# Weight preparation gets an order behind the operand splits on VectorE (attention and two MLPs, Trainium2)

## Chip, cores and metric

The kernel runs on one core of a Trainium2 chip. The metric is the device time of one execution in microseconds (us).

## What is computed

Attention over pooled keys and values, then two MLPs. The weights arrive as float64, whose bits the kernel decodes to float32; the rest is float32:

```python
k_p = k.reshape(B, H, Sp, 8, D).mean(axis=3)          # v_p alike; B = H = 8, S = 576, D = 64
attn = softmax(q @ k_p^T / sqrt(D))
x  = (attn @ v_p) -> [4608, 512]
x  = leaky_relu(x @ w_in1, 0.01) @ w_out1             # 512 -> 2048 -> 512
out = relu(x @ w_in2)**2 @ w_out2                     # 512 -> 2048 -> 512
```

## The kernel before

A float32 product is made from three matmuls of rounded operands: each operand is split into a high part (a cast on ScalarE, ACT) and a low part (operand minus high part, on VectorE, DVE), and `three()` (L302 to L304) multiplies high by high, high by low and low by high. So every operand of TensorE (PE) costs one ACT and one DVE instruction ahead of it: `split_weights` (L229, L230), `first` (`gh` L826, `gl` L827) and `split_into` (`oh`, `xh` L886; `ol`, `xl` L887).

Work runs in two stages.

**Stage 1: 80 units** (t, f). The first MLP is done plainly for the first 2304 tokens: five tiles t (four of 512 tokens, the last of 256) by 16 blocks f of hidden columns. Unit (t, f) traces `first` for the following unit, the weight splits, and `second`. Attention is interleaved (`advance`, three or five of its steps per unit) and is traced to its end in unit (3, 5). Two side jobs ride along:

- `prepare_sums` (`sums1`): 16 sets of sums of the first MLP's weights, two steps each (32 steps; L250 to L254), needed in stage 2. One step is traced in every odd unit from tile 1 on.
- `prepare_products` (`prep`): the second MLP's weights, 16 products (8 `in`, 8 `out`). A product has these steps: fetch; decode (ACT L192, then DVE L194 and L197, then L201, then L211, which is two half-size instructions in two steps for `out`); sums (four DVE instructions L250 to L254); high and low parts (ACT L291, DVE L292). That is 7 steps for `in`, 8 for `out`, 120 in all. Once attention has been traced, each unit takes three steps from `sums1`, and when that is exhausted from `prep` (one step per unit in tile 4, f < 6).

**Stage 2: nine passes** of 768 tokens with a seven-product (Strassen-like) scheme; passes 0 to 2 still belong to the first MLP, 3 to 8 are the second. A pass has two halves, `first2` and `second2`, of 28 **hooks** each. A hook is one product of one block: 12 matmuls in a half of passes 0 to 2. In a hook, `next_block` splits weight sums for blocks up to two hooks ahead (L940 ACT, L941 DVE); `second2` splits, after the matmuls of product k, block a, the operand that product k+1, block a needs four hooks later (`split_g`: L886, L887, for products 6 and 4 with a `minus` L890 ahead of them), and once per product a step of `products_x` for the next pass (`xl` L887, `xs` L890). `first2` calls `split_g` once in seven hooks. After each hook of number not divisible by 3 a step of `prep` is traced; the second MLP's first weight block may not be fetched before `prep` is exhausted.

The order on each engine is made ahead of time by a planner: of the instructions that its clock sees as ready it takes the one traced earliest. An instruction traced late therefore runs early wherever an engine is otherwise free. `add_manual_dep` with `NoSync` adds an edge to this plan, so that one instruction stands behind another on the same engine; it puts no semaphore wait into the program.

Of the kernel before, what the change touches and what calls it, by code (L numbers as in the profile page):

```python
# [20 lines left out]
TT = 512  # L21
# [6 lines left out]
def raw(ap):  # L28

    return ap.bitcast(F32)  # L30
# [3 lines left out]
def attention_two_mlps(  # L34
# [11 lines left out]
    nc = tc.nc  # L46
# [20 lines left out]
    WIDE = [min(TT, PLAIN - at) for at in range(0, PLAIN, TT)]  # L67
    NTILE = len(WIDE)
    NQ = NF // 2
# [37 lines left out]
    def behind(mark, n):  # L107

        traced, (end, last) = nc.cur_bb.bb.instructions, mark
        for ins in traced[end:end + n]:  # L110
            if ins.engine in last:
                tc.add_manual_dep(
                    ins, last[ins.engine].name,
                    mybir.DependencyInfo(mybir.DependencyClass.NoSync, mybir.DependencyReason.DATA),
                    reason="behind",
                )

    def temp(name, dt=F32):
        return tpool.tile([P, TT], dt, tag="t", name=name)

    def work(name, n=TT, early=False):
        if early:
            return ps_a.tile([P, n], F32, tag="acc", name=name)
        return ps_w.tile([P, n], F32, tag="w", name=name)
# [35 lines left out]
    def tick(n=1):  # L160

        for one in LATE:
            one[0] -= n
        while LATE and LATE[0][0] <= 0:
            nc.sync.dma_start(**LATE.pop(0)[1])
# [90 lines left out]
    def prepare_sums():  # L256

        for p in range(NQ):
            for kind in ("in", "out"):
                b = [[W[kind, p + i * NQ][:, j * HD:(j + 1) * HD] for j in range(2)] for i in range(2)]  # L260
                if kind == "out":
                    b = [[b[j][i] for j in range(2)] for i in range(2)]
                s = spool.tile([P, 4, HD], F32, tag="stage", name=f"s1_{kind}{p}")
                yield from sum_steps(s, *b[0], *b[1])
                later(2, out=WS[1, kind, p // 2][:, :, p % 2].rearrange("o p x -> p o x"), in_=s)
                yield
# [32 lines left out]
    def three(outp, a, b, first, last, **kw):  # L299

        (ah, al), (bh, bl) = a, b
        nc.tensor.matmul(outp, ah, bh, start=first, stop=False, **kw)  # L302
        nc.tensor.matmul(outp, ah, bl, start=False, stop=False, **kw)  # L303
        nc.tensor.matmul(outp, al, bh, start=False, stop=last, **kw)  # L304
# [478 lines left out]
    def put_stores(until):  # L783

        while STORES and STORES[0][0] <= until:
            nc.sync.dma_start(**STORES.pop(0)[1])
# [10 lines left out]
    def load_x(t):  # L797
        XS[t] = []
        for c in range(NK):
            st = temp(f"xs1_{t}_{c}")[:, :WIDE[t]]  # L800
            nc.sync.dma_start(out=st, in_=x0[t][c * P:(c + 1) * P, :])
            XS[t].append(st)

    def split_x(t):
        new_x(t)
        for (hi, lo), st in zip(X[1, t], XS.pop(t)):
            nc.scalar.copy(hi, st)
            nc.vector.tensor_tensor(out=lo, in0=st, in1=raw(hi), op=ALU.subtract)
# [4 lines left out]
    def first(t, f):  # L813

        x = X[1, t]
        wh, wl = HL.pop(("in", t, f))
        n = WIDE[t]
        h = work(f"h1_{t}_{f}")[:, :n]
        for c in range(NK):
            cs = slice(c * P, (c + 1) * P)  # L820
            three(h, (wh[:, cs], wl[:, cs]), x[c], c == 0, c == NK - 1)
        g = temp(f"g1_{t}_{f}")[:, :n]
        nc.scalar.activation(g, h, AF.Prelu, alpha=0.01)
        gh = gpool.tile([P, TT], F32R, tag="gh", name=f"gh1_{t}_{f}")[:, :n]
        gl = gpool.tile([P, TT], F32R, tag="gl", name=f"gl1_{t}_{f}")[:, :n]
        nc.scalar.copy(gh, g)  # L826
        nc.vector.tensor_tensor(out=gl, in0=g, in1=raw(gh), op=ALU.subtract)  # L827
        G[t, f] = (gh, gl)

    A = {}  # L830
# [11 lines left out]
    def second(t, f):  # L842
        gh, gl = G.pop((t, f))
        wh, wl = HL.pop(("out", t, f))
        if f == 0:
            A[t] = [ps_a.tile([P, TT], F32, tag="acc", name=f"acc1_{t}_{j}")[:, :WIDE[t]] for j in range(4)]
        acc = A[t]
        for j in range(4):
            js = slice(j * P, (j + 1) * P)
            three(acc[j], (wh[:, js], wl[:, js]), (gh, gl), f == 0, f == NF - 1)  # L850
        if f == NF - 1:
            for j in range(4):
                o = temp(f"o1_{t}_{j}")[:, :WIDE[t]]
                if j % 2 == 0:
                    nc.scalar.copy(o, acc[j])
                else:
                    nc.vector.tensor_copy(o, acc[j])
                store_x1(t, j, o)
# [26 lines left out]
    def split_into(hi, lo, src):  # L885
        nc.scalar.copy(hi, src)  # L886
        nc.vector.tensor_tensor(out=lo, in0=src, in1=raw(hi), op=ALU.subtract)  # L887

    def minus(out_, a, b):
        nc.vector.tensor_tensor(out=out_, in0=a, in1=b, op=ALU.subtract)  # L890
# [56 lines left out]
    def split_g(t, a, prod):  # L947

        g11, g12, g21, g22 = GF[t, a]
        src = {1: g11, 2: g21, 3: g22, 4: g11, 5: g11, 6: g11, 7: g12}[prod]  # L950
        if prod == 6:
            minus(g11, g22, g11)
        elif prod == 4:
            minus(g11, g21, g11)
        hi, lo = (gopool.tile([P, 2, HT], F32R, tag=g, name=f"{g}2_{t}_{a}_{prod}") for g in ("oh", "ol"))
        split_into(hi, lo, src)
        GO[t, a, prod] = (hi, lo)

    def square(g):
# [133 lines left out]
    prep, preparing, hooks = None, True, 0  # L1093
    sums1 = prepare_sums()

    def advance():
        nonlocal at_work, made
        made += 1
        if next(att, 1):
            at_work = False  # L1100
        put_stores(made - 2 if at_work else made)

    x2pool, xg = None, iter(())
    for i, (t, f) in enumerate(units):
        if f == NF - 3 and t + 1 < NTILE:
            while ready[0] * S < min((t + 2) * TT, PLAIN):
                advance()
            put_stores(made)
            load_x(t + 1)
        if f == NF - 1 and t + 1 < NTILE:  # L1110
            split_x(t + 1)

        rate = RATES[min(t, 1)]
        if i + 1 < len(units):
            first(*units[i + 1])
        tick()
        if i + 2 < len(units):
            split_weights("in", *units[i + 2])
        if i + 1 < len(units):
            split_weights("out", *units[i + 1])  # L1120
        while at_work and made < due + rate // 2:
            advance()
        second(t, f)
        tick()
        due += rate
        while at_work and made < due:
            advance()
        if w1 < NF:
            prepare_weights(w1)
            w1 += 1  # L1130
        elif t > 0 and f % 2:
            next(sums1, None)
        if not at_work:
            if prep is None:
                ppool = ctx.enter_context(tc.tile_pool(name="prep", bufs=1, side="right", reuse_waits="tile"))
                prep = prepare_products()
            for _ in range(3 if WIDE[t] == TT else 1 if f < NQ - 2 else 0):
                if preparing and next(sums1, 1) and next(prep, 1):
                    preparing = False
        if i == NF:  # L1140
            behind(marks[0], 3000)
        if t == NTILE - 1 and f >= NQ - 2:
            if x2pool is None:
                assert not at_work and next(sums1, 1)
                w_early_stack.close()
                x2pool = ctx.enter_context(tc.tile_pool(name="x2", bufs=1, side="right", reuse_waits="tile"))
                ring = ctx.enter_context(tc.tile_pool(name="ring", bufs=RING, side="right", reuse_waits="tile"))
                load_x2(0)
                tick(9)
                blocks.insert(0, next_block())  # L1150
            else:
                if not XO:
                    xg = products_x(0)
                next(xg, None)
# [7 lines left out]
    for t in range(LEAD + NPASS):  # L1162
        lead[0] = t < LEAD
        for half in (first2, second2):
            if half is second2 and t + 1 < LEAD + NPASS:
                load_x2(t + 1)
            for _ in half(t):
                tick()
                hooks += 1
                if hooks % 3 and preparing and next(prep, 1):  # L1170
                    preparing = False
                    tick(9)


# [27 lines left out]
```

## Time and profile before

| | us |
|---|---|
| median of 3 runs | 1655.0 (1651.8 to 1656.2) |
| the profiled execution | 1653.7 |
| its span, first to last instruction | 1652.0 |
| busy PE | 1612.2 (98%) |
| busy DVE | 1365.2 (83%) |
| busy ACT | 992.2 (60%) |
| busy POOL | 117.3 (7%) |

The shares are means over stages. A busy PE is one with a matmul under way; since records of matmuls overlap, the pace is read from their count in a window. Idle PE is where a term of the end time can be looked for.

### The profile page before, as it was taken

What the parts mean: (1) busy time and instruction counts of PE and PEld (TensorE: products, weight loads), DVE (VectorE), ACT (ScalarE), POOL (GpSimd) and SP (SyncE); (2) the same over time, 40 slices, a digit from 0 to 9 for tenths busy, and PEclk for the clock granted to TensorE, in tenths of its full rate; (3) what the DMA queues carried; (4) which work ended last, traced back from release to release, by engine and by line L of the source; (5) the groups of instructions that cost most, each with busy time, mean ns of one, the idle gap of its engine ahead of it and who ended that gap; (6) DMA issues with size and microseconds to landing.
All of it is one profiled execution on the core that took longest, in us unless ns stands there. A gap on an engine that the chain in (4) does not pass through costs nothing.

```text
span 1652.0 us, 27801 instructions
## 1 busy us (share of the span) xinstructions
PE 1612.2 (98%) x10040; PEld 1523.0 (92%) x10040; DVE 1365.2 (83%) x2057; ACT 992.2 (60%) x1779; POOL 117.3 (7%) x149
## 2 busy tenths in 40 slices
PE   5999999999999999999999999999999999999998
PEld 5777788888888999999999999999999999999998
DVE  5899899878689999978759589689689599698695
ACT  5778655655667868667556546456456455465454
POOL 3121232123210000000000000000000000000000
PEclk8999999999999999999999999999999999999999
DMA  7766556766347778886666755765766657556554
GB/s 180 200 191 183 170 168 189 232 193 200 120 143 268 273 251 286 280 297 214 226 194 204 236 184 168 261 195 176 245 188 205 225 175 240 197 176 212 188 187 140
DMA packets 223722, 341.07 MB, mean 206 GB/s; under 512 B 56160, under 2 KB 138080, under 8 KB 223584
## 3 DMA queue, kind: packets, MB, share of 16 engines
q1 hardware_dynamic: 223264, 338.76, 64.4%
q8 instruction: 80, 1.31, 0.3%
q10 hardware_dynamic: 320, 0.52, 0.1%
q14 instruction: 58, 0.48, 0.1%
HBM read 268.44 MB, written 69.21 MB: 204 GB/s over the span
## 4 chain that ended last, share of the span: by engine, by line
PE 82%; DVE 10%; DMA 3%; ACT 3%; issue 2%; SPq 1%; DVEq 0%; ACTq 0%
PE acc L302 13%; PE h L302 13%; PE acc L303 13%; PE acc L304 13%; PE h L304 13%; PE h L303 13%; PE s L532 1%; DVE gl L827 1%; DVE hl_in L230 1%; DMA xs<-x 1%; ACT x L549 1%; DVE hl_out L230 1%; DMA st_in_out<-in_moe_w_out_dram 1%; PE trq L511 1%; PE pt L582 1%
## 5 line engine op out<-in xcount | busy, mean ns | idle before, releaser
L302 PE MATMUL h<-xh,wb_in 128*128 128x384 f32 x1008 | 337.1, 334 | 0.9 <-DVE g L999 0.9
L303 PE MATMUL h<-xl,wb_in 128*128 128x384 f32 x1008 | 336.7, 334 | 0.0
L304 PE MATMUL h<-xh,wb_in 128*128 128x384 f32 x1008 | 336.7, 334 | 0.0
L886 ACT CAST oh<-g 128x768 fp32r<-128x768 f32 x252 | 210.5, 835 | 152.1 <-PE acc L303 89.6
L302 PE MATMUL acc<-wb_out,oh 128*128 128x256 f32 x1008 | 282.1, 280 | 0.0
L304 PE MATMUL acc<-wb_out,ol 128*128 128x256 f32 x1008 | 281.4, 279 | 0.0
L303 PE MATMUL acc<-wb_out,oh 128*128 128x256 f32 x1008 | 281.2, 279 | 0.0
L887 DVE TENSOR_TENSOR ol<-g,oh 128x768 fp32r<-128x768 f32 x252 | 239.3, 951 | 32.3 <-ACT oh L886 32.0
L302 PEld LDWEIGHTS h<-xh,wb_in 128*128 128x128 f32 x1008 | 189.2, 188 | 1.6 <-DVE g L999 1.4
L304 PEld LDWEIGHTS acc<-wb_out,ol 128*128 128x128 f32 x1008 | 189.4, 188 | 0.0
L303 PEld LDWEIGHTS h<-xl,wb_in 128*128 128x128 f32 x1008 | 189.2, 188 | 0.0
L304 PEld LDWEIGHTS h<-xh,wb_in 128*128 128x128 f32 x1008 | 189.2, 188 | 0.0
L302 PEld LDWEIGHTS acc<-wb_out,oh 128*128 128x128 f32 x1008 | 189.1, 188 | 0.0
L303 PEld LDWEIGHTS acc<-wb_out,oh 128*128 128x128 f32 x1008 | 188.7, 187 | 0.0
L941 DVE TENSOR_TENSOR wb_in<-wb_in 128x512 fp32r<-128x512 f32 x144 | 98.7, 687 | 91.4 <-ACT wb_in L940 87.0
L940 ACT CAST wb_in<-wb_in 128x512 fp32r<-128x512 f32 x144 | 89.2, 622 | 139.9 <-DMA wb_in<-ws_in 139.4
L890 DVE TENSOR_TENSOR g<-g,g 128x768 f32<-128x768 f32 x144 | 136.4, 950 | 1.8 <-ACT g L961 1.3
L302 PE MATMUL h<-xh,hl_in 128*128 128x512 f32 (+1 forms) x320 | 123.2, 385 | 7.1 <-ACT hl_in L229 5.6
L302 PE MATMUL acc<-gh,hl_out 128*128 128x512 f32 (+1 forms) x320 | 121.3, 386 | 2.8 <-ACT gh L826 2.8
L304 PE MATMUL h<-xh,hl_in 128*128 128x512 f32 (+1 forms) x320 | 119.8, 374 | 0.8 <-DVE hl_in L230 0.7
L303 PE MATMUL acc<-gl,hl_out 128*128 128x512 f32 (+1 forms) x320 | 118.8, 374 | 0.7 <-DVE gl L827 0.7
L303 PE MATMUL h<-xl,hl_in 128*128 128x512 f32 (+1 forms) x320 | 119.4, 373 | 0.0
(156 smaller groups left out, 3289.7 us busy)
## 6 DMA issues: line engine op xcount, KB each, us to landing
wb_in<-wd_in SPq DMA_DIRECT2D x108, 512.0 KB, 4.0
wb_out<-wd_out SPq DMA_DIRECT2D x108, 512.0 KB, 4.2
wb_in<-ws_in SPq DMA_DIRECT2D x144, 256.0 KB, 2.7
wb_out<-ws_out SPq DMA_DIRECT2D x144, 256.0 KB, 2.7
xs<-x SPq DMA_DIRECT2D x18, 768.0 KB, 4.7
out_dram<-o SPq DMA_DIRECT2D x24, 384.0 KB, 3.3
q<-in_q_dram SPq DMA_DIRECT2D x32, 256.0 KB, 4.2
v<-in_v_dram SPq DMA_DIRECT2D x64, 128.0 KB, 3.7
```

The source lines that it names most:

```text
L230: nc.vector.tensor_tensor(out=lo, in0=w, in1=raw(hi), op=ALU.subtract)
L302: nc.tensor.matmul(outp, ah, bh, start=first, stop=False, **kw)
L303: nc.tensor.matmul(outp, ah, bl, start=False, stop=False, **kw)
L304: nc.tensor.matmul(outp, al, bh, start=False, stop=last, **kw)
L511: nc.tensor.transpose(tr[:, m, :n], t[:n, 2 * m:2 * m + 2].rearrange("p a d -> p (a d)"), ident[:n, :n])
L532: nc.tensor.matmul(sc[:n, 2 * m:2 * m + 2].rearrange("p a x -> p (a x)"), qT[:, 2 * e + m, :n], kT[b % 2][:, 2 * e + m].rearrange("p a x - ...
L549: nc.scalar.activation(x[:n, 4 * e + h], sc[:n, h], AF.Exp, bias=mx[:n, h], accum_out=sm[:n, 4 * e + h],)
L886: nc.scalar.copy(hi, src)
L887: nc.vector.tensor_tensor(out=lo, in0=src, in1=raw(hi), op=ALU.subtract)
L890: nc.vector.tensor_tensor(out=out_, in0=a, in1=b, op=ALU.subtract)
L940: nc.scalar.copy(whole[:, 0], raw(whole[:, 1]))
L941: nc.vector.tensor_tensor(out=whole[:, 1], in0=raw(whole[:, 1]), in1=raw(whole[:, 0]), op=ALU.subtract)
```

## The change

Every DVE instruction that a step of `sums1` or `prep` traces gets an edge behind an anchor. The anchor is the last instruction traced by the latest `first` (`gl`) or `split_g` (`ol`). Steps per unit fall from three to two for tiles 0 to 3. ACT instructions and DMAs of a step get no edge. The order in which steps are traced stays.

```diff
+    def held(body):
+        traced = nc.cur_bb.bb.instructions
+        begin = len(traced)
+        body()
+        for ins in traced[begin:]:
+            if ins.engine == mybir.EngineType.DVE:
+                tc.add_manual_dep(
+                    ins, anchor[0].name,
+                    mybir.DependencyInfo(mybir.DependencyClass.NoSync, mybir.DependencyReason.DATA),
+                    reason="held",
+                )
+    anchor = [None]
...
         nc.vector.tensor_tensor(out=gl, in0=g, in1=raw(gh), op=ALU.subtract)
+        anchor[0] = nc.cur_bb.bb.instructions[-1]
...
         split_into(hi, lo, src)
+        anchor[0] = nc.cur_bb.bb.instructions[-1]
         GO[t, a, prod] = (hi, lo)
...
+    def prepare_step():
+        nonlocal preparing
+        if preparing and next(sums1, 1) and next(prep, 1):
+            preparing = False
+            tick(9)
...
         elif t > 0 and f % 2:
-            next(sums1, None)
+            held(lambda: next(sums1, None))
...
-            for _ in range(3 if WIDE[t] == TT else 1 if f < NQ - 2 else 0):
-                if preparing and next(sums1, 1) and next(prep, 1):
-                    preparing = False
+            for _ in range(2 if WIDE[t] == TT else 1 if f < NQ - 2 else 0):
+                held(prepare_step)
...
-                if hooks % 3 and preparing and next(prep, 1):
-                    preparing = False
-                    tick(9)
+                if hooks % 3:
+                    held(prepare_step)
```

## Rows read from the trace of the kernel before

**Rows 1.** The page: busy time, share of the span and instructions by engine.

```profile
PE 1612.2 (98%) x10040; PEld 1523.0 (92%) x10040; DVE 1365.2 (83%) x2057; ACT 992.2 (60%) x1779; POOL 117.3 (7%) x149
```

**Rows 2.** Busy time by engine in chosen windows: window, its length, then the columns named.

```profile
core 0: us, PE busy (x) PEld busy (x) DVE busy (x) ACT busy (x) POOL busy (x), PEclk, DMA share, GB/s
...
150.00:153.50 3.50, 0.01 (x1) 0.00 (x0) 3.10 (x6) 2.75 (x8) 0.75 (x1) 0.95 1.03 215
153.50:157.00 3.50, 3.48 (x9) 2.81 (x10) 3.44 (x6) 2.84 (x5) 1.80 (x3) 0.56 0.06 16
...
648.00:706.00 58.00, 58.00 (x335) 58.00 (x335) 57.90 (x79) 40.53 (x58) 0.00 (x0) 1.00 0.78 261
...
763.00:821.00 58.00, 58.00 (x337) 58.00 (x336) 50.19 (x63) 36.63 (x52) 0.00 (x0) 1.00 0.66 220
821.00:878.00 57.00, 57.00 (x331) 57.00 (x330) 31.95 (x39) 33.25 (x47) 0.00 (x0) 1.00 0.61 192
...
172.00:300.00 128.00, 124.28 (x663) 102.80 (x662) 119.64 (x266) 76.14 (x194) 35.19 (x40) 1.00 0.61 178
...
475.00:591.00 116.00, 112.46 (x681) 99.79 (x680) 112.18 (x200) 89.66 (x172) 2.10 (x3) 1.00 0.72 246
```

**Rows 3.** Instructions by tile: count, duration ns (min/median/max), first and last start.

```profile
L194 DVE TENSOR_SCALAR wm_in<-wm_in x8: 680/688/695, 315.9 to 704.3; 128x1024 f32<-128x1024 f32 x8
...
L201 DVE SCALAR_TENSOR_TENSOR wm_in<-st_in_in,wm_in x8: 1216/1224/1226, 317.4 to 705.7; 128x1024 uint32<-128x1024 uint32 x8
L211 DVE CUSTOM_DVE_ANT_0 ops_in<-wm_in,ops_in x8: 1215/1217/1218, 473.8 to 707.5; 128x2048 uint16<-128x2048 uint16 x8
...
L250 DVE TENSOR_TENSOR s_in<-ops_in x8: 414/416/426, 475.6 to 709.2; 128x256 f32<-128x256 f32 x8
...
L292 DVE TENSOR_TENSOR hl_in<-ops_in,hl_in x16: 412/552/693, 479.7 to 713.8; 128x512 fp32r<-128x512 f32 x8, 128x256 fp32r<-128x256 f32 x8
...
L292 DVE TENSOR_TENSOR hl_out<-ops_out,hl_out x16: 410/548/684, 489.4 to 739.5; 128x512 fp32r<-128x512 f32 x8, 128x256 fp32r<-128x256 f32 x8
...
L254 DVE TENSOR_TENSOR s_out<-w,s_out x8: 371/416/566, 187.5 to 289.6; 128x256 f32<-128x256 f32 x8
```

**Rows 4.** DVE in order of time, 625 to 745 us: start, duration, instruction.

```profile
643.86 0.42 DVE L253 TENSOR_TENSOR s_in<-s_in,ops_in 128x256 f32<-128x256 f32 x1
...
658.22 0.95 DVE L887 TENSOR_TENSOR ol<-g,oh 128x768 fp32r<-128x768 f32 x1
659.09 0.68 DVE L941 TENSOR_TENSOR wb_out<-wb_out 128x512 fp32r<-128x512 f32 x1
659.69 0.95 DVE L890 TENSOR_TENSOR g<-g,g 128x768 f32<-128x768 f32 x1
...
680.67 0.42 DVE L254 TENSOR_TENSOR s_in<-ops_in,s_in 128x256 f32<-128x256 f32 x1
```

**Rows 5.** The page's groups: count, busy us, mean ns, idle time before them.

```profile
L886 ACT CAST oh<-g 128x768 fp32r<-128x768 f32 x252 | 210.5, 835 | 152.1 <-PE acc L303 89.6
...
L887 DVE TENSOR_TENSOR ol<-g,oh 128x768 fp32r<-128x768 f32 x252 | 239.3, 951 | 32.3 <-ACT oh L886 32.0
```

**Rows 6.** DVE groups in 763 to 821 us, the x operands of the next pass.

```profile
L887 DVE TENSOR_TENSOR xl<-xs,xh 128x768 fp32r<-128x768 f32 x4 | 3.8, 948 | 0.0
...
L890 DVE TENSOR_TENSOR xs<-xs 128x768 f32<-128x768 f32 x1 | 0.9, 949 | 0.0
```

**Rows 7.** PE's waits: releaser, us in total, times, longest.

```profile
PE acc L302 <- ACT gh L826: 2.8, 3, 1.7
```

**Rows 8.** ACT and PE in order of time near 570 us, and the chain's DMA.

```profile
567.80 1.57 ACT L886 CAST xh<-xs 128x768 fp32r<-128x768 f32 x2 [2.67 <-DMA xs<-x]
...
570.51 0.38 PE L302 MATMUL acc<-gh,hl_out 128*128 128x256 f32 x1 [1.73 <-ACT gh L826]
...
559.53 10.33 DMA xs<-x
```

**Rows 9.** DVE and PE in order of time, 180 to 188 us.

```profile
180.72 1.49 DVE L250 TENSOR_TENSOR s_out<-w,w 128x256 f32<-128x256 f32 x1
...
187.47 0.40 PE L594 MATMUL pr<-ident,p 128*96 128x128 f32 x2 [2.00 <-ACT x L549]
```

## Prediction

> **What bounds the kernel now.** First the page's busy shares, then busy time in windows, then DVE in order of time where its windows are full. TensorE is busy for 98% of the span [rows 1]; all its idle time is 40 us, most of it before 172 us and after 1640 us, which the change does not reach. In the stretches that it touches there are 3.7 us idle from 172 to 300 us, where the sums run, and 3.5 us from 475 to 591 us, where the preparation is dense; in 648 to 706, 763 to 821 and 821 to 878 us there are none [rows 2]. So little can be gained, and what can be lost depends on how near VectorE is to holding TensorE up. It is full in 648 to 706 us (57.9 of 58), at 50.2 of 58 in the same half of the following pass, and at 32.0 of 57 in a first half [rows 2]: a second half is heavy, a first half light.
>
> Where the preparation runs now matters most. Its last instruction starts at 739.5 us and the last of the first sums at 289.6 us [rows 3]. By the code's count, steps are traced up to about hook 139, which at 12 matmuls of 58.0 / 337 = 172 ns [rows 2], 2.06 us a hook, from the start of the passes near 591 us would be about 878 us. The planner thus runs the steps up to 140 us ahead, into whatever room it finds. The timeline shows which room: the step whose third sum ran at 643.86 us got its fourth at 680.67 us, and between them stand only splits, back to back [rows 4]. A step ahead of its place gives way to every split.
>
> **What the change removes, adds and moves.** No instruction is added or removed: NoSync edges cost no time by themselves. It moves three things.
>
> *1. Sums of the first weights.* Traced over odd units of tiles 1 to 3, they now stay there: 8 of 32 steps in tile 1 rather than all of them before 290 us. A step is two instructions of 0.416 us [rows 3], so 24 steps, at most 20 us, leave a stretch in which DVE has 119.6 of 128 us [rows 2]. One stall shows how they hurt: 2.00 us at 187.5 us on exponentials, with a sum that took 1.49 us in DVE's queue shortly before [rows 9]. Gain: nothing if those exponentials were late anyway, 3.7 us if all idle time goes; the row shows a neighbour, not a cause, so I take 1. The sums land at 400 to 505 us, where the preparation has moved away; cost there nothing, and if that room is gone, 20 us of DVE work beside 116 us, still under its capacity.
>
> *2. Preparation in the last units.* Two steps a unit rather than three: the passes begin with 17 steps traced rather than 27. By order of products, about 65 steps had in truth run by 591 us, so some 48 leave the stretch 475 to 591 us. A product is, by the records, 0.69 + 0.69 + 1.22 + 1.22 + 4 x 0.416 + 2 x 0.55 = 6.6 us [rows 3]; 48 steps at 7.5 a product are about 40 us of DVE work. Their fetches and stores leave too, about 2.4 MB a product (1.05 in, 1.3 out, by tile sizes), 15 of the 28 MB that 246 GB/s for 116 us are [rows 2]. The idle time there is mostly 2.8 us of waiting for `gh` [rows 7]: ACT stood 2.67 us at `xh` for a load that took 10.33 us, and `gh` was queued behind it [rows 8]. With fewer DMAs beside it this load should land sooner. Gain between 0 (the load is late for its own stores) and 3.5 us; I take 2.5, as the wait has one visible cause that the change thins. Held DVE work does not hold the load itself. Further on, another 0 to 1 us in the first half of pass 0; I take 0.5.
>
> *3. The passes.* Here the price lies. 103 steps are now traced, and in second halves held, at two hooks in three up to about hook 154, so into the second half of pass 2. A traced step has the planner's rank of its place: ahead of all splits of later hooks. It no longer gives way, because it is no longer early.
>
> Cost of a step: records overlap, so I take start-to-start spacing: 0.87 us for an `ol` whose record is 0.95, 0.60 for a ring split of 0.68 [rows 4]. Ten instructions with 0.08 less each make a product 5.8 us, a step 0.78, and the 18.7 steps of a half 14.5 us. First half: 32 + 14.5 = 46.5 of 57.8 us (28 hooks); it fits. Second half: 50.2 + 14.5 = 64.7 of 57.8; it doesn't. By product (four hooks, 8.26 us of PE), with 0.87 for each split, difference, addition and x operation, 0.60 for each ring split, and 2.1 us of preparation: product 1, 5.5 + 2.1, less than 8.26; 5: 11.1 + 2.1, 4.9 over; 6 and 2: 6.4 + 2.1, 0.2 over each; 7: 8.5 + 2.1, 2.3 over; 3: 9.9 + 2.1, 3.7 over; 4: 2.3 + 2.1, 3.9 under. The backlog at the end of product 3 is 11.3 us. Two things eat into it. The x operations run ahead: only 5 of 11 stand in the second half of pass 1 [rows 6]; with the first half fuller I let 3 of these 6 stay ahead, 2.6 us. And the lead: an operand split after hook j is needed at hook j + 4, three hooks or 6.2 us, less 0.835 on ACT [rows 5] and 0.87 on DVE, and 0.87 more with a difference: 3.6 to 4.5 us; a ring split has two hooks and, behind a split and a step, as little as 1 us. I take 3.6, the heavy products' value. Loss: 11.3 - 2.6 - 3.6 = 5 us in each of passes 0 and 1; in pass 2, with steps for about 15 hooks, 5.3 - 2.6 + 1.9 - 3.6 = 1. Sum 11 us. Ends: 2.4 a half with all six ahead and 4.5 of lead (5 in all), 10.3 with none ahead and 1 of lead (24 in all).
>
> [...]
>
> DMAs and queues: fetches and stores of a step go through SP in order; a store that waits for a held step stands ahead of ring loads. The ring runs six blocks ahead, 12 us, more than any backlog above; cost nothing, and if that cover is gone, it is the backlog a second time, within the upper end. ACT parts of steps are not held, and ACT has room (36.6 of 58 [rows 2]).
>
> [...]
>
> **Sum.** Against the profiled execution of 1653.7 us (span 1652.0 and 1.7 around it): + 11 - 1 - 2.5 - 0.5 = + 7, 1660.7 us. The median of the runs shown is 1.3 us above that execution, so 1662.
>
> **Rivals.** *Faster: the lead holds.* The planner sees the load and lets x operations and ring splits run ahead in first halves, so the backlog stays under the lead; from about 8 us of work moved ahead per half on, the loss is nothing and the gains of 4 to 7 us are left: 1650. For it: 11 us of room in a first half, and second halves without preparation leave 8 us. Against it: x operands are free only when the pass's last products have read the old ones, and blocks have a ring of seven. *Even:* the loss is about 4 us, as large as the gains: 1655. [...] *The change does nothing:* in first halves the anchor moves once in seven hooks, so steps can still run ahead there; if the planner did the same as before, 1655. But steps ran up to 140 us ahead [rows 3], which an anchor at their own hook forbids.
>
> **How the numbers follow.** Slower as forecast 0.5, of which 0.1 is a net of under 5 us; much slower 0.1; even or without effect 0.2; faster 0.2, of which 0.05 gains too little to see. A measurement here tells 0.3%, 5 us, from no change: faster 0.15, same 0.35, slower 0.5. The range reaches from the faster rival's net of -7 to a net of 19: 1648 to 1674, which leaves out the largest losses and a gain beyond all idle time named.
>
> **What would show it.** Right: last preparation near 910 us rather than 740; TensorE waits of some microseconds on `ol`, ring splits or `g` in the second halves of passes 0 and 1 (after 648 and 763 us), DVE full there; hardly any idle before 591 us. Wrong: no new waits between 648 and 820 us; or new waits before 591 us, which nothing above allows for.

## The result and the profile after

The changed kernel takes 1664.1 us (median of 6 runs, 1660.1 to 1667.8) against 1654.9 us before: ratio 1.0059, 95% interval 1.0048 to 1.0069. It is slower by 9 us; the forecast was 1662. In the changed file `three()` stands at L317 to L319, `gl` at L842, `oh`/`ol` at L902/L903, ring splits at L956/L957.

The profiled execution (1662.4 us, span 1660.6 against 1652.0) begins with the page's busy times, which [rows 1] answer to, and shows nothing by itself: every engine does the same work.

```profile
PE 1615.8 (97%) x10040; PEld 1522.0 (92%) x10040; DVE 1359.8 (82%) x2057; ACT 987.0 (59%) x1779; POOL 116.6 (7%) x149
```

Where the time went is read from landmarks. The matmuls on a ring block appear on fixed tiles, `wb_in` in first halves and `wb_out` in second halves, and their first and last start bound each half: a second half runs from the first start to the last, a first half fills the time between. For the second half of pass 0 the rows of before and after, in that order, are (start of the first and of the last of 112):

```profile
L302 PE MATMUL acc<-oh,wb_out x112: 331/335/335, 650.0 to 707.7; 128*128 128x384 f32 x112
```

```profile
L317 PE MATMUL acc<-oh,wb_out x112: 331/336/441, 648.5 to 711.3; 128*128 128x384 f32 x112
```

57.7 us have become 62.8. All halves of passes 0 to 2 read in this way, for all kernels of this study (each from its profiled execution, us; the last matmul of pass 2's second half closes the passes, and from there to the end of the span every kernel takes 711 to 713 us):

| kernel | passes start | 0 first | 0 second | 1 first | 1 second | 2 first | 2 second | passes 0 to 2 |
|---|---|---|---|---|---|---|---|---|
| before | 590.6 | 59.4 | 57.7 | 58.8 | 57.7 | 58.8 | 57.7 | 350.1 |
| changed | 588.2 | 60.3 | 62.8 | 58.5 | 61.2 | 60.3 | 58.1 | 361.2 |
| e1, edges in units alone | 588.7 | 60.1 | 57.7 | 61.3 | 57.7 | 64.3 | 57.8 | 358.9 |
| e2, edges in hooks alone | 587.7 | 60.8 | 63.1 | 58.5 | 61.6 | 63.1 | 58.1 | 365.2 |
| e3, no edges | 589.7 | 59.7 | 57.7 | 59.1 | 57.7 | 58.8 | 57.7 | 350.7 |
| e4, ring split earlier | 590.2 | 60.0 | 63.2 | 58.1 | 60.5 | 59.0 | 58.7 | 359.5 |
| e5, light places | 589.2 | 61.9 | 58.1 | 58.9 | 61.0 | 62.3 | 57.7 | 359.9 |
| e7, e1 with few fetches | 589.5 | 60.8 | 57.7 | 62.8 | 57.7 | 62.8 | 57.8 | 359.6 |
| e8, more steps, edges | 614.9 | 59.7 | 57.7 | 59.9 | 57.7 | 58.8 | 57.7 | 351.5 |
| e9, changed with few fetches | 588.8 | 58.7 | 61.7 | 59.3 | 61.5 | 60.0 | 58.2 | 359.4 |
| e10, more steps, no edges | 591.7 | 59.9 | 57.7 | 60.4 | 57.7 | 58.7 | 57.8 | 352.2 |
| e12, changed with less DVE | 588.2 | 59.0 | 57.7 | 59.5 | 57.7 | 60.7 | 57.8 | 352.4 |
| e13, e1 with less DVE | 587.5 | 61.5 | 57.7 | 60.0 | 57.7 | 63.1 | 57.7 | 357.7 |
| e14, e1 with less ACT | 590.0 | 59.1 | 57.7 | 60.2 | 57.7 | 61.9 | 57.7 | 354.3 |

The change gains 2.4 us ahead of the passes and loses 11.1 in them: 9.0 in second halves (5.1, 3.5, 0.4), 2.1 in first halves (0.9, -0.3, 1.5).

Each row of the table is one execution, up to 2.4 us away from the median of its kernel, and not every column is equally firm. Second halves without edges in the hooks take 57.7 or 57.8 us in all eight kernels of that kind, so a loss there is read to some tenths. First halves differ without any edge: e10 takes 2.0 us more for its three than the kernel before. The starts of the passes scatter as well, 589.7 to 591.7 us in the three kernels without edges (mean 590.7) and 587.7 to 590.2 in the six with edges in the hooks (mean 588.7). So the gain ahead of the passes is about 2 us, and a loss of 2 us in first halves is no more than e10 shows.

The windows of the changed kernel, to be held against [rows 2] (window, length, PE, PEld, DVE, ACT, POOL busy with counts, granted clock, DMA share, GB/s):

```profile
172.00:300.00 128.00, 123.60 (x658) 101.96 (x658) 99.55 (x214) 75.51 (x193) 33.81 (x39) 1.00 0.45 127
...
475.00:591.00 116.00, 115.62 (x704) 103.65 (x703) 88.39 (x163) 72.71 (x145) 2.10 (x3) 1.00 0.49 167
```

Between 475 and 591 us VectorE's work fell from 112.2 to 88.4 us, traffic from 246 to 167 GB/s, TensorE's idle time from 3.5 to 0.4 us. Between 172 and 300 us VectorE lost 20 us of sums, and TensorE gained nothing: 4.4 us idle instead of 3.7. By halves, in the same columns, pass 0's second half, pass 1's and the first half of pass 2 before the change, then the changed kernel's passes 0 and 1:

```profile
650.00:707.70 57.70, 57.70 (x335) 57.70 (x334) 57.60 (x79) 38.67 (x55) 0.00 (x0) 1.00 0.78 262
...
766.50:824.20 57.70, 57.70 (x334) 57.70 (x334) 46.69 (x59) 33.41 (x48) 0.00 (x0) 1.00 0.67 218
824.20:883.00 58.80, 58.80 (x342) 58.80 (x341) 36.95 (x44) 37.56 (x53) 0.00 (x0) 1.00 0.63 197
```

```profile
588.20:648.50 60.30, 58.84 (x339) 58.20 (x338) 46.31 (x65) 40.23 (x58) 0.00 (x0) 1.00 0.81 273
648.50:711.30 62.80, 60.34 (x341) 58.75 (x339) 60.83 (x87) 42.05 (x62) 0.00 (x0) 1.00 0.86 277
...
769.80:831.00 61.20, 59.19 (x336) 57.89 (x336) 59.89 (x86) 41.99 (x62) 0.00 (x0) 1.00 0.86 280
```

A second half now holds 60 to 61 us of VectorE work, more than the 57.7 us that TensorE needs for it; the first half beside it holds 46. The 62.8 us contain 341 matmuls and not 335: six of the next first half run at 706.8 to 707.8 us, ahead of this half's last. So about 1 us of the 9.0 belongs to first halves, and the 11.1 us are about 8 and 3.

The preparation, which ended at 739.5 us [rows 3], is spread to 924 us:

```profile
L307 DVE TENSOR_TENSOR hl_out<-ops_out,hl_out x16: 418/554/691, 554.7 to 924.1; 128x512 fp32r<-128x512 f32 x8, 128x256 fp32r<-128x256 f32 x8
```

Who is waited for stands in the waits of TensorE's weight loads, 588 to 950 us (releaser, us in total, times, longest):

```profile
PEld acc L319 <- DVE wb_out L957: 5.5, 7, 1.5
PEld h L317 <- DVE g L1016: 3.0, 4, 0.8
PEld acc L317 <- ACT oh L902: 1.4, 2, 1.1
PEld h L317 <- ACT s L1006: 1.3, 1, 1.3
PEld acc L318 <- DVE ol L903: 0.7, 1, 0.7
PEld h L319 <- DVE wb_in L957: 0.4, 2, 0.2
```

7.6 of these 12.3 us belong to `acc`, the second halves; before, the whole list for the passes (590.6 to 941 us) was one wait in a first half:

```profile
PEld h L302 <- DVE g L999: 1.2, 1, 1.2
```

The weight-load row is the better one here. TensorE's own idle time adds up to 7.2 us only, since a matmul's record is 0.34 us long (the rows above) while the next starts 0.17 us after it (57.7 us for 335), so that it runs on for about 0.16 us and hides the beginning of each gap.

How one of them comes about is seen on VectorE between 665 and 672 us (start, duration, instruction):

```profile
665.53 0.69 DVE L209 TENSOR_SCALAR wm_out<-wm_out 128x1024 f32<-128x1024 f32 x1
666.13 0.95 DVE L906 TENSOR_TENSOR g<-g,g 128x768 f32<-128x768 f32 x1
667.00 0.69 DVE L212 TENSOR_SCALAR wm_out<-wm_out 128x1024 uint32<-128x1024 uint32 x1
667.61 0.69 DVE L957 TENSOR_TENSOR wb_out<-wb_out 128x512 fp32r<-128x512 f32 x1
668.21 0.95 DVE L903 TENSOR_TENSOR ol<-g,oh 128x768 fp32r<-128x768 f32 x1
669.08 1.22 DVE L216 SCALAR_TENSOR_TENSOR wm_out<-st_out_out,wm_out 128x1024 uint32<-128x1024 uint32 x1
670.21 0.95 DVE L906 TENSOR_TENSOR g<-g,g 128x768 f32<-128x768 f32 x1
671.08 1.29 DVE L957 TENSOR_TENSOR wb_out<-wb_out 128x512 fp32r<-128x512 f32 x2
```

and TensorE behind it:

```profile
671.82 0.44 PE L319 MATMUL acc<-oh,wb_out 128*128 128x384 f32 x1 [1.12 <-DVE wb_out L957]
```

VectorE never pauses, and three pieces of a decode (`wm_out`) stand among the splits, where before there was no preparation for 37 us [rows 4]. The ring split at 671.08 us is late by 1.12 us.

### The profile page after: what moved, and what is told of

Read it like the earlier page. It is cut to its first block, busy times and chain, and to the rows that moved or that the text cites. A ratio compares the mean times of both kernels' runs of the same rounds, so it can differ in the third digit from the quotient of the medians.

```text
span 1660.6 us, 27809 instructions
## 1 busy us (share of the span) xinstructions
PE 1615.8 (97%) x10040; PEld 1522.0 (92%) x10040; DVE 1359.8 (82%) x2057; ACT 987.0 (59%) x1779; POOL 116.6 (7%) x149
## 4 chain that ended last, share of the span: by engine, by line
PE 75%; DVE 13%; ACT 4%; DMA 4%; issue 2%; SPq 0%; ACTq 0%; POOL 0%; DVEq 0%; POOLq 0%
PE h L317 12%; PE h L319 12%; PE h L318 12%; PE acc L317 11%; PE acc L319 11%; PE acc L318 11%; DVE ol L903 2%; DMA wb_in<-ws_in 2%; PE s L547 1%; ACT x L564 1%; DVE wb_out L957 1%; PE trq L526 1%; DVE xl L903 1%; DMA st_in_out<-in_moe_w_out_dram 1%; DVE g L906 1%
## 5 line engine op out<-in xcount | busy, mean ns | idle before, releaser
L317 PE MATMUL h<-xh,wb_in 128*128 128x384 f32 x1008 | 338.0, 335 | 2.8 <-DVE g L1016 1.8
L319 PE MATMUL h<-xh,wb_in 128*128 128x384 f32 x1008 | 337.2, 335 | 0.0
L902 ACT CAST oh<-g 128x768 fp32r<-128x768 f32 x252 | 210.2, 836 | 153.2 <-PE acc L318 93.8
L317 PE MATMUL acc<-wb_out,oh 128*128 128x256 f32 x1008 | 282.5, 280 | 0.0
L319 PE MATMUL acc<-wb_out,ol 128*128 128x256 f32 x1008 | 281.8, 280 | 0.0
L903 DVE TENSOR_TENSOR ol<-g,oh 128x768 fp32r<-128x768 f32 x252 | 239.9, 955 | 27.4 <-ACT oh L902 26.8
L317 PEld LDWEIGHTS h<-xh,wb_in 128*128 128x128 f32 x1008 | 189.3, 188 | 4.7 <-DVE g L1016 3.3
L319 PEld LDWEIGHTS acc<-wb_out,ol 128*128 128x128 f32 x1008 | 189.8, 188 | 0.0
L319 PEld LDWEIGHTS h<-xh,wb_in 128*128 128x128 f32 x1008 | 189.3, 188 | 0.4 <-DVE wb_in L957 0.4
L317 PEld LDWEIGHTS acc<-wb_out,oh 128*128 128x128 f32 x1008 | 189.2, 188 | 0.0
L956 ACT CAST wb_in<-wb_in 128x512 fp32r<-128x512 f32 x144 | 89.1, 621 | 137.0 <-DMA wb_in<-ws_in 127.0
L957 DVE TENSOR_TENSOR wb_in<-wb_in 128x512 fp32r<-128x512 f32 x144 | 98.4, 688 | 75.1 <-ACT wb_in L956 66.4
L317 PE MATMUL h<-xh,hl_in 128*128 128x512 f32 (+1 forms) x320 | 123.6, 386 | 9.2 <-ACT hl_in L244 6.0
L319 PE MATMUL h<-xh,hl_in 128*128 128x512 f32 (+1 forms) x320 | 120.3, 376 | 0.7 <-DVE hl_in L245 0.6
L317 PE MATMUL acc<-gh,hl_out 128*128 128x512 f32 (+1 forms) x320 | 120.7, 385 | 0.1
```

Source lines behind the costliest of these rows:

```text
L956: nc.scalar.copy(whole[:, 0], raw(whole[:, 1]))
L957: nc.vector.tensor_tensor(out=whole[:, 1], in0=raw(whole[:, 1]), in1=raw(whole[:, 0]), op=ALU.subtract)
```

## The experiments

### Which edges, and is it the edges at all

In the diffs below a line of three dots stands for lines left out, and some calls are shortened.

e1 keeps the edges of the units and takes those of the hooks away; e2 does the reverse; e3 has none and keeps only the smaller number of steps a unit.

```diff
-            held(lambda: next(sums1, None))      # e2, e3
+            next(sums1, None)
...
-                held(prepare_step)               # in the units: e2, e3
+                prepare_step()
...
                 if hooks % 3:
-                    held(prepare_step)           # in the hooks: e1, e3
+                    prepare_step()
```

> The edges stay in the units of stage 1 (sums and preparation there); the steps traced in the hooks of the passes have none. Two steps a unit, as in the changed kernel. My theory: the loss comes from preparation that is held in second halves, where VectorE has no room; without the hold it runs ahead into first halves again and gives way. Passes 0 to 2, from the first matmul on a ring block to the last of pass 2's second half, then take about 350 us as before (changed kernel 361), the passes start near 588 us, time about 1652 us. Rival, later start: with 17 instead of 27 steps traced ahead, and with none running ahead in stage 1, too much is left for the passes whatever the hold: passes 356 us or more, time 1658 us or more.

Measured: 1659.6 us, ratio 1.0031 (1.0018 to 1.0044). My expectation of 1652 was wrong and the rival's 1658 or more right: second halves are back at 57.7, exactly as long as before, but first halves lose 0.7, 2.5 and 5.5 us. Its halves from 706.5 us on:

```profile
706.50:767.80 61.30, 59.73 (x342) 58.77 (x341) 52.62 (x74) 45.22 (x65) 0.00 (x0) 1.00 0.95 322
767.80:825.50 57.70, 57.70 (x335) 57.70 (x334) 56.27 (x75) 37.31 (x54) 0.00 (x0) 1.00 0.76 250
825.50:889.80 64.30, 59.57 (x340) 58.57 (x339) 51.34 (x74) 44.95 (x65) 0.00 (x0) 1.00 0.91 305
```

Without edges in the hooks the planner fills the second halves of passes 0 and 1 to 56 of 57.7 us. The rest goes to first halves, and there TensorE waits although VectorE has 9 us or more to spare.

> The reverse: edges only on steps traced in the hooks of the passes, none in stage 1. My theory: passes 0 to 2 about 361 us as in the changed kernel; passes start near 590 us as before or up to 2 us earlier, because of the 103 held steps none can run in stage 1 any more, so the stretch 475 to 591 us is as thin as in the changed kernel; time 1662 to 1666 us. Rival: if the gain in stage 1 came from the hold on the sums, the passes start at 590 to 591 us; if from the thinned preparation, at 588 to 589 us.

Measured: 1665.3 us, ratio 1.0061 (1.0046 to 1.0077). Second halves lose 5.4, 3.9 and 0.4 us, as in the changed kernel, so the edges in hooks make that loss. First halves lose 1.4, -0.3 and 4.3 us, with the same edges in the hooks as the changed kernel, which shows how little one execution fixes them; in the last of them the granted clock was 0.97. The passes start at 587.7 us, as early as in the changed kernel, without an edge on the sums; these ran early again, as VectorE's 118.0 us show:

```profile
172.00:300.00 128.00, 124.27 (x655) 102.79 (x655) 118.01 (x264) 74.59 (x192) 33.62 (x39) 0.99 0.60 176
475.00:587.70 112.70, 112.32 (x685) 100.31 (x684) 74.51 (x127) 70.89 (x142) 2.10 (x3) 1.00 0.33 107
```

So the gain ahead of the passes belongs to the thinned preparation, and ordering the sums brought nothing that shows: 3.7 us idle with early sums here, 3.7 before, 4.4 with held ones.

> No edges at all; only the smaller number of steps a unit is left of the change. My theory: the planner runs steps ahead as before, the last preparation lands near 740 us, passes start near 590.6 us, passes 0 to 2 take 350 us, time 1653 to 1657 us. Rival: if the number of steps a unit matters by itself (rank of the steps among the last units), the time is 1659 us or more.

Measured: 1654.8 us, ratio 0.9999 (0.9989 to 1.0008), passes 350.7 us, last preparation at 739.4 us. The smaller number of steps a unit does nothing by itself.

### Steps in the places that have room

e5 leaves every edge in and traces the steps of the passes elsewhere:

```diff
-                if hooks % 3:
+                place_ = (hooks - 1) % 56
+                n_steps = 1 if place_ < 32 else 2 if place_ >= 52 else 0
+                for _ in range(n_steps):
                     held(prepare_step)
```

> All edges as in the changed kernel, but steps are traced in other hooks of the passes: one in each of a first half's 28 hooks and of product 1's four in a second half, two in each of product 4's last four, none in between. The number of steps and the work are the same. My theory (no room in the middle of second halves): first half 32 + 28 x 0.78 = 54 of 58 us, second half with steps only where VectorE is below TensorE; the loss falls from 11 us to 0 to 3 us, time 1651 to 1655 us. Rival (the hold itself costs, wherever the step stands, because held steps wait in a full queue): passes 0 to 2 stay at 357 us or more, time 1659 us or more.

Measured: 1661.6 us, ratio 1.0042 (1.0030 to 1.0054): the rival's side. Pass 0's second half loses 0.4 us instead of 5.1, as expected of a half without steps in its middle, but pass 1's still 3.3, and first halves lose 2.5, 0.1 and 3.5. In pass 1's the pieces of a decode and its sums, traced, by the code's count, by the end of product 1 (8 us into the half), ran until 783 us, 15 us into it: a held step can also come late, and then it stands in the middle all the same. One first half took the whole load for 0.1 us (54.3 us of VectorE work in 58.9), two others did not (50.2 in 61.9, 54.6 in 62.3); room on VectorE alone did not decide these first halves.

### Is it VectorE's work in second halves

e4 splits ring blocks one hook earlier (`NEAR = 4`), so the split that is late first gets 2 us more.

> The changed kernel with ring blocks split up to three hooks ahead instead of two (NEAR = 4). My theory: in second halves the queue on VectorE is too long in sum, and the ring split is only the first to be late because it has the thinnest cover (TensorE waits on wb_out first); with one hook more, 2.06 us, it is late by less: the 9 us lost in the second halves of passes 0 to 2 fall by 2 to 5 us, time 1658 to 1662 us. Rival (the sum alone decides, the wait just moves to ol): passes 0 to 2 stay at 360 us or more, time 1663 to 1666 us.

Measured: 1661.0 us, ratio 1.0032 (1.0020 to 1.0045), 3 us less than the changed kernel, the time of my theory; its passes of 359.5 us lie near the rival's 360. Second halves still lose 5.5, 2.8 and 1.0. The waits of the weight loads, 590 to 950 us, have moved in part as the rival says, from the ring split (5.5 us in the changed kernel, 0.5 now) to the operand splits:

```profile
PEld acc L317 <- ACT oh L902: 2.8, 3, 1.5
PEld h L317 <- DVE g L1016: 2.6, 4, 0.9
PEld acc L318 <- DVE ol L903: 2.0, 4, 0.8
...
PEld acc L319 <- DVE wb_out L957: 0.5, 1, 0.5
```

Of the 5.0 us that the ring split lost, 2.7 came back on `oh` and `ol` (2.1 us in the changed kernel, 4.8 now); all waits on `acc` went from 7.6 to 5.3. So more cover for one consumer helped here by about half, and the next in line was late for the rest. The passes fell by 1.7 us in this execution; that this is where the 3 us of the median come from, it does not show.

e12 takes VectorE's work away instead: the changed kernel without the clamps and the merge of the second MLP's decode.

```diff
+        full = name.startswith("1_")
+        if full:
             nc.vector.tensor_scalar(out=raw(m), ..., op0=ALU.max, op1=ALU.min)
             nc.vector.tensor_scalar(out=m, ..., op0=ALU.logical_shift_left, op1=ALU.bitwise_and)
         yield
+        if full:
             nc.vector.scalar_tensor_tensor(out=m, in0=high, ..., op1=ALU.bitwise_or)
```

> The changed kernel without three of the ten or eleven VectorE instructions of a product (the clamps and the merge of the decode, 0.69 + 0.69 + 1.22 of 6.6 us; the decoded weights are wrong, all else stays). My theory: second halves lose because VectorE's work there is larger than TensorE's; preparation falls from 2.1 to 1.3 us per product of four hooks, the backlog of 11.3 us to 6.3, of which run-ahead and lead take 6.2, so the second halves of passes 0 to 2 lose 0 to 2 us instead of 9, passes take 350 to 354 us, time 1650 to 1656 us. Rival (waits of held steps on their ScalarE parts or loads): second halves lose 6 us or more, time 1659 us or more.

Measured: 1655.6 us, ratio 1.0001 (0.9990 to 1.0012). Second halves lose 0.0, 0.0 and 0.1 us. All edges are in place and the held steps still wait for their loads and ScalarE parts; VectorE's sum per second half has gone below TensorE's 57.7:

```profile
647.20:704.90 57.70, 57.70 (x334) 57.70 (x334) 56.30 (x81) 41.84 (x61) 0.00 (x0) 1.00 0.87 280
...
764.40:822.10 57.70, 57.70 (x335) 57.70 (x334) 56.86 (x82) 42.10 (x62) 0.00 (x0) 1.00 0.88 287
```

56 to 57 us cost nothing here (before, pass 0 held 57.6 without loss), 60 to 61 cost 3.5 to 5.1 in the changed kernel: its loss in second halves is VectorE's queue, and 8.6 of the 9.0 us stand in the two halves whose work is above TensorE's time. The sum does not give its size: pass 1 of e5 held 58.4 us and lost 3.3, so it also matters where in the half the work stands. First halves still lose -0.4, 0.7 and 1.9.

### What makes first halves late

Four runs ask this. e7 is e1, e9 the changed kernel, with the second MLP's weights fetched for the first product of each kind alone; e13 is e1 without the three VectorE instructions that e12 leaves out; e14 is e1 without two ScalarE pieces of a product.

```diff
-                st = fetch_weights(2, [(kind, p), (kind, p + NQ)])       # e7, e9
+                if p == 0:
+                    kept[kind] = fetch_weights(2, [(kind, p), (kind, p + NQ)])
+                st = kept[kind]
```

```diff
-        else:
+        elif name.startswith("1_"):                                      # e14
             nc.scalar.activation(raw(m), raw(high), AF.Abs)
...
-            out=raw(m), in0=raw(m), ...
+            out=raw(m), in0=raw(m if name.startswith("1_") else high), ...
...
-            nc.scalar.activation(r, low, AF.Copy, scale=2.0 ** -29)
-            nc.vector.tensor_tensor(out=r, in0=m, in1=r, op=ALU.add)
+            if name.startswith("1_"):
+                nc.scalar.activation(r, low, AF.Copy, scale=2.0 ** -29)
...
+            else:
+                nc.vector.tensor_tensor(out=raw(r), in0=raw(m), in1=raw(m), op=ALU.add)
```

> As the run with edges in the units alone, which took 359 us for passes 0 to 2 and lost 9 us in first halves only; here the second MLP's weights are fetched for the first product of each kind alone and every later product decodes the same ones, so 14 of 16 fetches of 1.05 MB and the right weights are left out; every decode, sum, split and store stays. Theory now: in first halves the DMA queues are nearly full (305 to 322 GB/s), ring loads land late, and ScalarE, in order, holds the casts for them ahead of the copies that TensorE waits for. Without 15 of 34 MB of preparation traffic passes 0 to 2 take 350 to 353 us, time 1650 to 1654 us. Rival (VectorE or ScalarE work of the 48 steps more, whatever the traffic): passes stay at 357 us or more, time 1657 us or more.

Measured: 1662.5 us, ratio 1.0049 (1.0031 to 1.0067), first halves lose 1.4, 4.0 and 4.0. Between 591 and 950 us the traffic fell from 284 (e1) to 252 GB/s and the loss did not: my account by nearly full DMA queues falls for e1, at least as far as fetches go.

> The changed kernel with the fetch left out as in the run above (later products decode the first ones' weights again). Theory now: its 9 us in second halves are VectorE's queue and stay, the 2 us in first halves are the DMA's and go: passes 0 to 2 at 357 to 360 us, time 1659 to 1663 us. Rival (all of it is traffic): passes 353 us or less, time 1656 us or less.

Measured: 1658.8 us, ratio 1.0024 (1.0013 to 1.0036). Second halves lose 4.0, 3.8 and 0.5 us (8.3 of 9.0 stay), first halves -0.7, 0.5 and 1.2, together 1.0 instead of 2.1. That is on the theory's side, but a difference of 1 us in first halves is too small to hang a cause on, beside e7. The median says more than the profile: 1.0024 against the changed kernel's 1.0059, intervals apart, is some 6 us, while the profiled execution, 2.4 us above its own median, is only 1.2 us shorter than the changed kernel's. By the medians the fetches thus have a part in the changed kernel's loss that the one profile does not show; where it lies stays open.

> The kernel with edges in the units alone, which lost 9 us in first halves, without the same three VectorE instructions of a product. If VectorE, filled to the brim by unheld steps, is what makes first halves late, passes 0 to 2 fall from 359 to 350 to 353 us, time 1650 to 1654 us. If it is ScalarE's in-order queue (casts that wait for ring loads and pieces of preparation ahead of the copies that TensorE waits for), first halves still lose 5 us or more, time 1656 us or more.

Measured: 1657.1 us, ratio 1.0010 (0.9997 to 1.0022), first halves lose 2.1, 1.2 and 4.3, 7.6 us together of 8.7 in e1. In the last of them VectorE is busy for 41.7 of 63.1 us, and the granted clock was below full:

```profile
824.40:887.50 63.10, 60.59 (x341) 60.27 (x339) 41.71 (x54) 41.17 (x60) 0.00 (x0) 0.97 0.81 259
```

TensorE waited up to 2.8 us there for one copy of ScalarE, and behind that wait the granted clock was 0.57 from 832 to 835 us and 0.86 from 835 to 838: 1.7 us of full clock (the row's 0.97 over 63.1 us comes to 1.9), a good part of this half's 4.3. e7 has 0.97 in the same half, e1 and e14 1.00.

> The kernel with edges in the units alone, without two of the four ScalarE pieces of a product's preparation (absolute value and scaled low words, 2.3 of 3.4 us on ScalarE; VectorE's instructions keep their number and size; the decoded weights are wrong). If ScalarE's queue makes first halves late, they lose 4 us or less of the 9 and the time is 1650 to 1655 us. If not, they lose 6 us or more, time 1657 us or more.

Measured: 1658.1 us, ratio 1.0025 (1.0013 to 1.0037), first halves lose -0.3, 1.4 and 3.1, 4.2 us together: half of e1's, between the two expectations (4 or less, 6 or more); the time is on the side of the second (1657 or more). What TensorE waits for in e1 (588 to 948 us) is mostly ScalarE's copies out of PSUM:

```profile
PEld h L317 <- ACT s L1010: 4.3, 3, 1.9
PEld h L317 <- ACT s L1006: 3.9, 2, 2.7
PEld h L317 <- DVE g L1016: 1.9, 2, 1.3
```

and ScalarE, in order of time ahead of the longest of them, shows what stands in front of that copy:

```profile
825.76 1.16 ACT L207 ACTIVATE wm_out<-st_out_out 128x1024 f32<-128x1024 f32 x1 [2.84 <-DVE ops_in L226]
828.17 0.62 ACT L306 CAST hl_in<-ops_in 128x512 fp32r<-128x512 f32 x1 [1.26 <-DMA wd_out<-hl_out]
...
831.03 0.62 ACT L956 CAST wb_in<-wb_in 128x512 fp32r<-128x512 f32 x1 [1.02 <-DMA wb_in<-ws_in]
831.56 0.40 ACT L306 CAST hl_in<-ops_in 128x256 fp32r<-128x256 f32 x1
831.86 0.79 ACT L1006 COPY s<-h 128x768 f32<-128x768 f32 x1
```

ScalarE waited 2.84 us for VectorE's decode, 1.26 for an earlier store, 1.02 for a ring block, one after the other, with the copy queued behind all of it. That is shown for this one copy. Which kind of work makes first halves late is not: by halves of one execution, e14 takes away 4.5 us of e1's 8.7 and e13 1.1, but over all runs e13 (1.0010) is nearer to the kernel before than e14 (1.0025), whose interval overlaps e1's almost wholly. Leaving out the fetches brought nothing in e1 (e7). The cause, and why one first half of e5 goes free, stays open.

### Edge or rank

e8 and e10 trace five steps a unit in tile 3 and three in tile 4, so that 59 instead of 17 stand ahead of the passes; e8 is e1 with this, e10 is e3 with it.

```diff
-            for _ in range(2 if WIDE[t] == TT else 1 if f < NQ - 2 else 0):
+            for _ in range(5 if WIDE[t] == TT else 3 if f < NQ - 2 else 0):
```

> Edges in the units alone, but five steps a unit in tile 3 and three in tile 4, so that by the code's count 59 of 120 steps are traced ahead of the passes, nearly as many as ran there before the change (about 65). Theory now: the loss is the 48 steps moved into the passes, not the edge as such; with them back, passes 0 to 2 take 350 to 353 us; the stretch 475 to 591 us is dense again, passes start at 589 to 592 us; time 1653 to 1657 us. Rival (an edge costs by itself): passes stay at 356 us or more, or stage 1 loses more than 3 us, time 1659 us or more.

Measured: 1681.8 us, ratio 1.0166 (1.0142 to 1.0191). Both expectations got one half: with the steps back in stage 1 the passes take 351.5 us, so what they lost was the work moved into them; and the edge costs by itself, 24 us in stage 1.

> As the run with five and three steps a unit, which lost 24 us in 475 to 615 us, but with no edges anywhere. Separates edge from rank: in both kernels 59 steps are traced ahead of the passes, here they may run earlier. If the edge costs (a step may not use room ahead of its unit, so it comes in one lump with the splits of that unit), stage 1 is back at 589 to 592 us and the time at 1653 to 1657 us. If the rank costs (steps traced early go ahead of the splits of later units), the loss stays: passes start after 605 us, time 1670 us or more.

Measured: 1656.4 us, ratio 1.0008 (0.9996 to 1.0020), passes start at 591.7. Same steps, same trace order, no edge: the 24 us are gone. The stretch from 475 us to the start of the passes, e8 above e10:

```profile
475.00:614.90 139.90, 123.31 (x681) 105.97 (x681) 120.19 (x220) 89.20 (x171) 2.10 (x3) 0.94 0.71 238
```

```profile
475.00:591.70 116.70, 114.79 (x693) 101.69 (x692) 114.49 (x202) 91.30 (x175) 2.10 (x3) 1.00 0.73 247
```

In e8 VectorE has 120.2 us of work here, more than the 115.6 us that the stretch took before; the last of the held sums ran at 505 us in e8, in e10 at 292. The excess of work alone is some 5 us. By TensorE's side, 13 us of the 24 are idle time (16.6 us instead of 3.5), and the granted clock, 0.94 over 139.9 us, is another 8 us of full clock. The longest group of TensorE's waits in the stretch (releaser, us in total, times, longest):

```profile
PE acc L318 <- DVE gl L842: 8.2, 5, 4.6
```

Ahead of the 4.6 us wait VectorE ran nothing but held steps from 536.4 to 539.9 us, and only then the `gl`; the granted clock from 540 to 545 us was 0.66. So held steps came in a bunch ahead of the following unit's split here, and the longest wait cost clock as well.

## Why the prediction was right

**The bound.** That the matter would be decided by VectorE in second halves, and that steps had been running ahead into first halves and stage 1, held: e3 and e10 put them ahead again and are as fast as before. Between the two sums of [rows 4] stood not only splits, as I read it, but also the differences and additions that belong to them; no preparation did, and that is what the argument needs.

**Sums.** The gain of 1 us is the step that failed in stage 1: idle time there went from 3.7 to 4.4 us, and e2 shows the same 3.7 with early sums. The stall in [rows 9] did shrink, from 2.0 us to 0.2 at that matmul, but a wait of 1.8 us for the same exponentials came at another matmul, at 195 us. The lower bound, nothing, was right.

**Preparation in the last units.** Gain forecast 2.5 us; the passes start 2.4 us earlier in the profiled pair, 2.0 by the means above. The wait for `gh` [rows 7] is gone, and `xh` no longer waits for the load of [rows 8]. All that TensorE still waits for between 475 and 591 us is:

```profile
PE acc L318 <- DVE gl L842: 0.3, 1, 0.3
```

**Second halves.** Forecast 5, 5 and 1; measured 5.1, 3.5 and 0.4, of which about 1 us belongs to first halves. The cause is shown (e2 against e1, and e12). Of the terms, the windows were cut 3.5 us early: bounded by the halves' own landmarks, pass 1's second half held 46.7 us of VectorE work before, not 50.2, and a first half 37.0, not 32.0. With 14.5 us of steps that is 61.2, and 60.8 and 59.9 were measured. Two terms were wrong by about the same amount and cancelled. I had let 3 x operations, 2.6 us, run ahead; in the changed kernel six of the eleven stand ahead of pass 1's second half (769.8 us), 5.2 us. The first and the last of the six, and the next one:

```profile
760.65 0.95 DVE L903 TENSOR_TENSOR xl<-xs,xh 128x768 fp32r<-128x768 f32 x1
...
767.46 0.95 DVE L903 TENSOR_TENSOR xl<-xs,xh 128x768 fp32r<-128x768 f32 x1
771.96 0.95 DVE L903 TENSOR_TENSOR xl<-xs,xh 128x768 fp32r<-128x768 f32 x1
```

And I had taken a cover of 3.6 us, that of operand splits; late first was the ring split, which I had put at as little as 1 us, and with more cover the next in line was (e4). With these two, 11.3 - 5.2 - 1 is again 5: the mechanism was right, its figure partly luck. The lower end of the span was also added up wrong: all six ahead and 4.5 of lead leave 1.6 a half, not 2.4. No bound of the range hangs on it.

**First halves.** Here the sum was wrong: "it fits", with a gain of 0.5. It fits on VectorE (46 to 50 us of 58), but 2.1 us were lost, about 3 with the six matmuls counted here, on waits for `g` and ScalarE's copies (3.0 and 1.3 us of the weight loads' waits). I had granted ScalarE room by its share (36.6 of 58 us) and did not ask what stands ahead of a copy in its queue. e1, where the steps of the hooks go to first halves, loses 8.7 us there. So the 11.1 us of the passes are about 8 of the predicted kind and about 3 of one that I had priced at nothing; the total of 11 came out so close because the errors cancelled. How firm the 3 us are, e2 (5.4 us in first halves) and e10 (2.0 without any edge) show: not very.

**Rivals.** *Faster* had its mechanism in part: all six x operations ran ahead, but ring splits did not (16 on `wb_out` in pass 1's second half, before and after), and 5.2 us fell short of the 8 that it asked for. The much slower kernel, given a chance of 0.1, did not come about; e8 (1681.8 us) is one, where edges meet a full stretch, with waits of up to 4.6 us and a granted clock of 0.94. The forecast's sum has no term for the clock, and in the changed kernel's passes it was 1.00 in every half; that it can fall there too, e2, e7 and e13 show with 0.97 in one first half each.

## What to carry to other kernels

An order edge that keeps filler work (work that the planner lets everything else pass) from running early also keeps it out of the gaps that hid it; before adding one, sum the engine's work by the stretch in which the held work will now fall, cut at the consumer's own landmarks, and compare it with the bound engine's time there. Giving one consumer more lead did not take the wait away where a stretch was over that time by 2 to 4 us: one hook more, 2 us, moved 2.7 of 5.0 us to the next consumer (e4). And a share of busy time says little about a queue whose order is fixed ahead (ScalarE was busy for 41.2 of 63.1 us in the half of e13 in which one of its copies came 2.8 us late): look at what stands ahead of the instruction that the bound engine waits for.

## What was not expected of the hardware

A second half could be filled to 57.6 of 57.7 us on VectorE (pass 0 before; 56.9 in e12) without a matmul being late. Above that the price rose fast: 58.4 us cost 3.3 us (e5, pass 1), 59.9 and 60.8 cost 3.5 and 5.1 (the changed kernel, passes 1 and 0).

A wait of 2 to 3 us on TensorE did not always cost clock. Behind waits of 2.8 us in e13 and 2.3 to 2.6 us in e2 and e7 the granted clock of that first half was 0.97; behind one of 2.7 us in e1 it stayed at 1.00. Three of the fourteen profiled executions lost some 1.9 us of full clock each in this way in the passes (0.97 over 63 us), as much as many of the differences between first halves.
